# Moving the regrouping of k and q and the order of the loads in an attention and mixer kernel

## The chip, the core and the metric

The kernel runs on one core of a Trainium2 chip. Its time is the device time of one execution in microseconds (us). A comparison takes the median of several runs. The five engines of the core each work through a list of instructions in the order written: PE (the matrix engine, with its weight loads shown apart as PEld), DVE (the vector engine), ACT (the scalar engine), POOL (GpSimd) and SP, which here only issues transfers. An instruction waits at the head of its list until what it reads is there and what it overwrites is free, and all that stands behind it on that engine waits with it.

## What is computed

Sigmoid attention over 8 batches, 12 heads, 448 positions and 64 values a head, followed by a mixer block on the result:

```python
scores = (1 / sqrt(64)) * matmul(q, k.transpose(0, 1, 3, 2)) - log(448)
attn_out = matmul(1 / (1 + exp(-scores)), v)          # [8, 12, 448, 64]
x = attn_out.transpose(0, 2, 1, 3).reshape(8, 448, 768)
h = maximum(x.transpose(0, 2, 1) @ w_tok1, 0) @ w_tok2
u = x + h.transpose(0, 2, 1)
out = u + maximum(u @ w_ch1, 0) @ w_ch2               # float32
```

`w_tok1` is 448x256, `w_tok2` 256x448, `w_ch1` 768x1536 and `w_ch2` 1536x768.

## The kernel before

**Cycles.** The work runs in 24 cycles, `c = 3 * b + u`: batch `b` from 0 to 7, and `u` from 0 to 2, each a unit of four heads. In cycle `c` PE makes the scores of unit `c` (seven calls of `qk`, one for each `j`), the values of unit `c - 1` (`av`), the token step of unit `c - 2` (`tok_tail`, `tok1`, `ytrans`), and, as filling between them, the channel step of an earlier batch: the second product of batch `b - 2` in every cycle (`ch2_pair`, `pieces_last`) and the first product of batch `b - 1` at the end of each third cycle (`sevens`). This steady order holds from cycle 9 (`ONE_RUN`) on. Cycles 6 to 8 go through the same steps with a list `pending` of pieces of the channel step of batch 0 (`work`), and what comes before is an opening of its own. The schedule is written out by hand: the order of calls in the program is the order on each engine.

**How k and q get to PE.** `load` (lines 110 to 118) is issued on POOL, as two transfers a tensor and batch, which also turn float32 into float16; the bytes land in `raw_k`, `raw_q` (one buffer each) or `raw_v` (two). `relayout` (120) copies a unit of `raw_k` or `raw_q` into `rel_k` or `rel_q` on DVE, three copies a tensor and batch. `dma_transpose` (138) is one transfer from SP that transposes the three units into `tr_k` or `tr_q`, which `qk` reads. `through_dma` (144) gives the eight pieces of a batch as a list: three copies and the transpose of k, then three copies and the transpose of q. The list `copies` is emptied at places that the code names: in the steady cycles `some(within)` stands after the third `qk`, ahead of `av`, and `some(behind)` stands after the channel step's `rest()`, ahead of `ytrans`.

**What else stands on DVE.** `av` ends in two copies `xa` to `xT` (line 220) and a small one (226); `ytrans` (305) ends in the two additions to `ut` (319); `rest` ends in additions into `outs` (564); `sevens` has the additions and the clamp at lines 521 and 524; `token_sums` (434) makes four tiles `diffs` a batch. The first two matter here: `av` and `ytrans` both use the PSUM banks 0 and 1 (`at_bank[0] = Y`), and so does `tok_tail`. The next user of a bank waits on PE until DVE (or ACT, for `tk`) has emptied it.

**What else stands on SP.** The transpose of `xT` into `xn` (`xtrans_dma`, 235), that of `ut` into `un` (`utrans`, 324), and the stores.

**When the loads go out.** `gated_loads(b)` (969) is called near the end of a batch's second or third cycle. Its first instruction is a small copy on POOL that reads the last piece of `tr_q` of batch `b + 1`, so POOL waits until that transpose has landed and then issues `load` for v of batch `b + 1` and for k and q of batch `b + 2`. Line 1038 does a like thing once, at the end of cycle 5. In the steady cycles the calls are at line 1144 (cycle 11) and at line 1167 (cycles 13, 16, 19).

**In the last batch** (`b == 7`) there is no batch to follow, and `copies` holds twelve sums of `c2` made on DVE (`output_sums`, 620) for the last part of the program.

Of the kernel before, what the change touches and what calls it, by code (L numbers as in the profile page):

```python
# [23 lines left out]
NU = 3  # L24
# [6 lines left out]
def kernel(  # L31
# [11 lines left out]
    nc = tc.nc  # L43

    B, H, S, E = q.shape
# [24 lines left out]
    gate = pc.tile([128, 2], FP16, name="gate")  # L70
# [24 lines left out]
    att, xn, h1, un = {}, {}, {}, {}  # L95
# [14 lines left out]
    def load(b, t, src, u0, u1):  # L110

        for g in range(2):
            dst = raw_tile(b, t)[64 * g : 64 * g + 64, u0:u1, :, :, :]
            heads = src[b, 6 * g + 2 * u0 : 6 * g + 2 * u1]
            nc.gpsimd.dma_start(
                out=dst.rearrange("p u hi j e -> p (u hi) (j e)"),
                in_=heads.rearrange("h (p j) e -> p h (j e)", j=NJ),
            )
# [25 lines left out]
    def through_dma(b, u0):  # L144

        pieces = []
        for t in ("k", "q"):
            for u in range(u0, NU):
                pieces.append(lambda t=t, u=u: relayout(b, t, u))
            pieces.append(lambda t=t: dma_transpose(b, t, u0))  # L150
        return pieces
# [27 lines left out]
    def qk(b, u, j):  # L179
        att[b, u, j] = pa.tile([128, 2, S], FP16, tag="att", bufs=10, name=f"att_{b}_{u}_{j}")  # L180
        ps = pp.tile([128, 2, 512], FP32, tag="qk", bufs=2, name=f"qk_{b}_{u}_{j}")
        for g in range(2):
            for hi in range(2):
                nc.tensor.matmul(  # L184
                    out=ps[64 * g : 64 * g + 64, hi, 0:S],
                    lhsT=tr[b, "k"][64 * hi : 64 * hi + 64, u, j, 64 * g : 64 * g + 64],
                    rhs=tr[b, "q"][64 * hi : 64 * hi + 64, u, :, 64 * g : 64 * g + 64],
                    start=True,
                    stop=True,
                )  # L190
        nc.scalar.activation(  # L191
            out=att[b, u, j][:, :, :],
            in_=ps[:, :, 0:S],
            func=SIGMOID,
            bias=bias_t[:, :],
            scale=att_scale,
        )
# [37 lines left out]
    def xtrans_dma(b, u):  # L235
        nc.sync.dma_start_transpose(
            out=xn_tile(b, u).rearrange("s g t d -> s (g t) d"),
            in_=xTs[b % 2][:, u, :, :].rearrange("d g s -> d (g s)"),
        )
# [65 lines left out]
    def ytrans(b, u, banks=()):  # L305
        for g in range(2):
            db = NU * g + u
            if banks:
                at_bank[0] = banks[g]
            ps = bank([128, 512], FP32, f"yt_{b}_{db}")  # L310
            for tcb in range(2):
                nc.tensor.matmul(  # L312
                    out=ps[:, 0:S],
                    lhsT=h1[b, u][:, tcb, g, :],
                    rhs=w2[:, tcb, :, :],
                    start=(tcb == 0),
                    stop=(tcb == 1),
                )
            nc.vector.tensor_tensor(  # L319
                out=uts[b % 2][:, db, 0:S], in0=xTs[b % 2][:, u, g, 0:S], in1=ps[:, 0:S], op=ADD  # L320
            )
# [79 lines left out]
    def weight_sums():  # L401

        low, high = slice(0, NU), slice(NU, NDB)
        first, second = slice(0, MC), slice(MC, CC)
        s1, s2, s4 = sums

        def one(out, in0, in1, op):
            return [
                lambda d=d: nc.vector.tensor_tensor(
                    out=out[:, d, :], in0=in0[:, d, :], in1=in1[:, d, :], op=op  # L410
                )
                for d in range(NU)
            ]

        return [
            *one(s1, c1[:, high, second], c1[:, low, second], ADD),
            *one(s2, s1, c1[:, low, first], SUB),
            *one(s4, c1[:, high, first], s2, SUB),
            *one(c1[:, low, second], c1[:, low, first], c1[:, low, second], SUB),
        ]  # L420
# [350 lines left out]
    for g, queue in enumerate((nc.scalar, nc.sync)):  # L771
        queue.dma_start(
            out=first_q[64 * g : 64 * g + 64].rearrange("p hi j e -> p hi (j e)"),
            in_=q[0, 6 * g : 6 * g + 2].rearrange("h (p j) e -> p h (j e)", j=NJ),
# [28 lines left out]
    for par in range(2):  # L803
        part = slice(64 * par, 64 * par + 64)
        nc.gpsimd.dma_start(
            out=w1[part, 0:3, :],
            in_=tok_rows[0:6].rearrange("(t par) p c -> par p t c", par=2)[par],
# [161 lines left out]
    def gated_loads(b):  # L969

        nc.gpsimd.tensor_copy(  # L971
            out=gate[:, :], in_=tr[b + 1, "q"][:, NU - 1, NJ - 1, 126:128]
        )
        if b > 1:
            load(b + 1, "v", v, 0, NU)
        for t, src in (("k", k), ("q", q)):
            if b + 2 < B:
                load(b + 2, t, src, 0, NU)

    ON_DMA = range(N_FIRST, N_CYCLES)  # L980

# [68 lines left out]
                copies.pop(0)()  # L1050

    pending, copies = [], []
    early = weight_sums()
    lane = [0]
    for c in range(2 * NU, ONE_RUN):
        b, u = divmod(c, NU)
        before, ahead = divmod(c - 1, NU), divmod(c - 2, NU)


        if c == 2 * NU:  # L1060
            first = c
            pending, shares = [*pieces_ch2(0, by_half[2:]), *pieces_last(0)], [10, 10, 10]
            total = sum(w for w, f in pending)
            spent = 0

        def work(share):
            goal = 3 * sum(shares[: c - first]) + share * shares[c - first]
            done = 0
            while pending and spent + done < total * goal / 90:
                w, f = pending.pop(0)  # L1070
                if len(pending) % 4 == 3:
                    lane[0] ^= 1
                at_bank[0] = 2 + lane[0]
                f()
                done += w
                if copies:
                    copies.pop(0)()
                elif early:
                    early.pop(0)()
            return done  # L1080

        qk(b, u, 0)
        qk(b, u, 1)
        at_bank[0] = 0
        av(*before)
        xtrans_dma(*before)
        qk(b, u, 2)
        if c == 2 * NU + 2:
            copies += through_dma(3, 0)[NU + 1 :]
        spent += work(1)  # L1090
        qk(b, u, 3)
        qk(b, u, 4)
        at_bank[0] = 0
        tok_tail(*ahead)
        tok1(*ahead, with_scores=True)
        if c == 2 * NU + 1:
            copies = through_dma(3, 0)[: NU + 1]
        spent += work(2)
        if c == 2 * NU + 2:
            utrans(b - 1)  # L1100
            token_sums(b - 1)
        qk(b, u, 5)
        qk(b, u, 6)
        if u < 2:
            at_bank[0] = 0
            ytrans(*ahead)
        spent += work(3)
        if u == 2:
            sevens(b - 1)
            at_bank[0] = 0  # L1110
            ytrans(*ahead)
            gated_loads(b)
    assert not copies and not pending and not early

    def some(n):
        for f in copies[:n]:
            f()
        del copies[:n]

    for c in range(ONE_RUN, N_CYCLES):  # L1120
        b, u = divmod(c, NU)
        before, ahead = divmod(c - 1, NU), divmod(c - 2, NU)
        if b == NU:
            within, behind = ((0, 0), (4, 2), (2, 0))[u]
        else:
            within, behind = 2, 2
        if u == 0:
            assert not copies
            copies += through_dma(b + 1, 0) if b + 1 < B else output_sums()

        X, Y = 2, 0
        at_bank[0] = X
        turn0, turn1, rest = ch2_pair(b - 2, u)
        part = len(turn1) * 2 // 3
        qk(b, u, 0)
        qk(b, u, 1)
        for f in turn0:
            f()  # L1140
        qk(b, u, 2)
        some(within)
        if c == ONE_RUN + 2:
            gated_loads(b)
        if u == 2:
            utrans(b - 1)
        at_bank[0] = Y
        av(*before, 0, 4)
        qk(b, u, 3)
        av(*before, 4, NJ)  # L1150
        xtrans_dma(*before)
        if u == 2:
            token_sums(b - 1)
        qk(b, u, 4)
        for f in turn1[:part]:
            f()
        qk(b, u, 5)
        for f in turn1[part:]:
            f()
        at_bank[0] = Y  # L1160
        tok_tail(*ahead)
        qk(b, u, 6)
        tok1(*ahead, with_scores=True)
        rest()
        some(behind)
        if u == 1 and NU < b < B - 1:
            gated_loads(b)
        if u == 2:
            at_bank[0] = Y + 1
            for w, f in pieces_last(b - 2):  # L1170
                f()
            sevens(b - 1)
        at_bank[0] = Y
        ytrans(*ahead)
    assert not copies


# [90 lines left out]
```

## The time and the profile before

| | |
|---|---|
| runs | 345.99, 347.44, 349.06 us; median 347.44 us |
| profiled execution | 347.11 us, of which the span from the first to the last instruction is 345.3 us |
| busy share of the span | PEld 70%, DVE 62%, ACT 61%, POOL 16% |
| loads from POOL | 41.5% of the 16 transfer engines' time |
| transposes and stores from SP | 49.2% of it |
| waits of PE for another engine, all together | 2.5 us |
| waits of POOL for `tr_q` to land (its gate copies) | 153.0 us at line 971, 14.0 us at line 1038 |
| one copy of `relayout` (line 126) | 611 ns alone, 1.14 us for two in a row |
| one addition to `ut` (line 319) | 614 ns alone, 1.15 us for two in a row |

In the profile a line of a timeline gives the start, the duration, the engine, the line of the program, the operation with what it writes and reads, how many in a row, and in brackets how long the engine had sat idle before and who released it. The ends of the matrix instructions are modelled, and an instruction of PE that waits for its bank can be shown as a longer one. So a wait of PE is better read from the distance between the starts of like steps in two cycles than from PE's idle time.

### The profile page before, as it was taken

The page shows a single profiled execution, that of the slowest core. Times are in us where ns is not written, and L with a number is a line of the kernel's source. Part 1 is how long each engine was busy: PE and PEld are TensorE (multiplying, and loading weights), DVE is VectorE, ACT ScalarE, POOL GpSimd, SP SyncE. Part 2 cuts the span into 40 slices and gives each one's busy share as a digit, 9 for nine tenths or more (in the row PEclk, how much of TensorE's full clock was granted, in tenths as well). Part 3 has the DMA queues.
Part 4 walks back from the last instruction along what each step waited for, and adds up shares of the span by engine and source line. Part 5 has one row for each costly group of instructions (what it writes and reads, how often), then busy time and mean ns, then how long its engine had stood idle before and what let it go on. Part 6 is the DMA issues. An engine that isn't in the chain of part 4 may idle for free.

```text
span 345.3 us, 10256 instructions
## 1 busy us (share of the span) xinstructions
PE 338.2 (98%) x4465; PEld 241.5 (70%) x4465; DVE 213.7 (62%) x427; ACT 210.9 (61%) x271; POOL 56.7 (16%) x98
## 2 busy tenths in 40 slices
PE   7999999999999999999999999999999999999994
PEld 4555556555886679766896669766896779767962
DVE  2377466577775665756575654765665684976662
ACT  3996846487748865788448865688448875111400
POOL 8982440230040013000400013000100000000000
PEclk9999999999999999999999999999999999999999
DMA  7999999999999999989997999979963592035406
GB/s 120 174 170 189 208 203 203 169 175 219 200 181 205 198 184 208 153 126 164 181 228 87 165 193 156 199 108 170 176 135 30 82 171 68 1 78 128 79 2 159
DMA packets 104380, 52.17 MB, mean 151 GB/s; under 512 B 76432, under 2 KB 101264, under 8 KB 104336
## 3 DMA queue, kind: packets, MB, share of 16 engines
q1 hardware_dynamic: 78944, 29.70, 49.2%
q0 software_dynamic: 25168, 21.50, 41.5%
q8 instruction: 35, 0.57, 0.7%
q10 hardware_dynamic: 224, 0.33, 0.4%
q14 instruction: 9, 0.07, 0.1%
HBM read 43.45 MB, written 11.01 MB: 158 GB/s over the span
## 4 chain that ended last, share of the span: by engine, by line
PE 88%; ACT 4%; DMA 3%; DVE 2%; issue 1%; POOL 0%; DVEq 0%; ACTq 0%
PE c_ab L491 14%; PE c L367 12%; PE qk L184 9%; PE c_c L491 8%; PE xa L211 8%; PE c L605 6%; PE tk L289 5%; PE c L734 5%; PE yt L312 5%; PE c L541 4%; ACT att L191 4%; PE c L695 4%; PE c L344 3%; DMA raw_k<-in_k_dram 2%; DMA first_q<-in_q_dram 1%; PE c_b L491 1%
## 5 line engine op out<-in xcount | busy, mean ns | idle before, releaser
L191 ACT ACTIVATE att<-qk,att_bias 128x896 f16<-128x896 f32 x168 | 155.3, 1015 | 34.0 <-PE qk L184 33.7
L184 PE MATMUL qk<-tr_q,tr_k 64*64 64x448 f16 x672 | 59.5, 359 | 0.3 <-ACT att L191 0.2
L491 PEld LDWEIGHTS <-c 128*128 128x128 f16 x504 | 47.8, 98 | 1.9 <-issue 1.8
L367 PE MATMUL c<-c,h 64*64 64x384 f16 x960 | 47.1, 322 | 0.0
L220 DVE CAST xT<-xa 128x448 f16<-128x448 f32 x48 | 27.7, 620 | 31.1 <-PE xa L211 31.0
L211 PE MATMUL xa<-att,raw_v 64*64 64x448 f16 x672 | 40.3, 349 | 0.1
L512 ACT ACTIVATE pt_ab<-c_ab 128x896 f32<-128x896 f32 x21 | 19.3, 917 | 30.8 <-PE c_ab L491 30.8
L367 PEld LDWEIGHTS <-h 64*64 64x64 f16 x960 | 29.5, 107 | 11.0
L491 PEld LDWEIGHTS <-sum 128*128 128x128 f16 x378 | 36.3, 98 | 0.0
L184 PEld LDWEIGHTS <-tr_k 64*64 64x64 f16 x672 | 21.5, 105 | 19.2 <-issue 11.9
L564 DVE TENSOR_TENSOR o<-un,c 128x384 f32<-128x384 f16 x34 | 18.8, 554 | 23.9 <-PE c L605 20.6
L319 DVE TENSOR_TENSOR ut<-xT,yt 128x448 f16<-128x448 f16 x48 | 27.5, 614 | 2.5 <-PE yt L312 2.5
L211 PEld LDWEIGHTS <-raw_v 64*64 64x64 f16 x672 | 21.5, 107 | 10.6 <-issue 1.0
L971 POOL COPY gate<-tr_q 128x2 f16<-128x2 f16 x6 | 1.1, 184 | 153.0 <-DMA tr_q<-rel_q 153.0
L303 ACT ACTIVATE h<-tk 128x256 f16<-128x256 f32 x42 | 14.3, 412 | 14.8 <-PE tk L289 14.8
L541 PE MATMUL c<-c,h 128*128 128x384 f16 x120 | 22.3, 326 | 0.0
L312 PE MATMUL yt<-w,h 128*128 128x448 f16 x96 | 22.1, 353 | 0.0
L605 PE MATMUL c<-c,h 128*128 128x384 f16 x120 | 22.0, 326 | 0.0
L514 ACT ACTIVATE h<-c_ab 128x896 f16<-128x896 f32 x7 | 6.4, 917 | 24.4 <-PE c_ab L491 24.4
L289 PE MATMUL tk<-xn,w 128*128 128x256 f16 x156 | 21.2, 274 | 0.1
L521 DVE TENSOR_TENSOR h<-pt_c,c_c 128x448 f16<-128x448 f32 x21 | 13.0, 617 | 13.2 <-PE c_c L491 13.2
L521 DVE TENSOR_TENSOR h<-pt_ab,c_ab 128x896 f16<-128x896 f32 x14 | 15.2, 1084 | 9.6 <-PE c_ab L491 9.6
(100 smaller groups left out, 461.4 us busy)
## 6 DMA issues: line engine op xcount, KB each, us to landing
out_dram<-o SPq DMA_DIRECT2D x48, 192.0 KB, 2.9
c<-in_moe_w_ch_dram POOLq DMA_DIRECT2D x4, 1152.0 KB, 15.9
raw_k<-in_k_dram POOLq DMA_DIRECT2D x10, 336.0 KB, 10.8
raw_q<-in_q_dram POOLq DMA_DIRECT2D x10, 336.0 KB, 13.7
raw_v<-in_v_dram POOLq DMA_DIRECT2D x10, 336.0 KB, 8.0
out_dram<-o SPq DMA_DIRECT2D x15, 96.0 KB, 6.9
raw_q<-in_q_dram POOLq DMA_DIRECT2D x12, 112.0 KB, 5.0
raw_k<-in_k_dram POOLq DMA_DIRECT2D x12, 112.0 KB, 4.8
```

Source lines behind the costliest of these rows:

```text
L184: nc.tensor.matmul(out=ps[64 * g : 64 * g + 64, hi, 0:S], lhsT=tr[b, "k"][64 * hi : 64 * hi + 64, u, j, 64 * g : 64 * g + 64], rhs=tr[b, " ...
L191: nc.scalar.activation(out=att[b, u, j][:, :, :], in_=ps[:, :, 0:S], func=SIGMOID, bias=bias_t[:, :], scale=att_scale,)
L211: nc.tensor.matmul(out=ps[g][64 * hi : 64 * hi + 64, 0:S], lhsT=raw[b, "v"][64 * g : 64 * g + 64, u, hi, j, :], rhs=att[b, u, j][64 * g : ...
L220: nc.vector.tensor_copy(out=xTs[b % 2][:, u, g, 0:S], in_=ps[g][:, 0:S])
L289: nc.tensor.matmul(out=ps[tcb], lhsT=w1[rows, t, cols], rhs=xn[b, u][rows, :, t, :], start=(t == 0 and not with_scores), stop=(t == (2 if ...
L312: nc.tensor.matmul(out=ps[:, 0:S], lhsT=h1[b, u][:, tcb, g, :], rhs=w2[:, tcb, :, :], start=(tcb == 0), stop=(tcb == 1),)
L319: nc.vector.tensor_tensor(out=uts[b % 2][:, db, 0:S], in0=xTs[b % 2][:, u, g, 0:S], in1=ps[:, 0:S], op=ADD)
L367: nc.tensor.matmul(out=ps[p][m : m + 64, 0:n], lhsT=lhsT(p, part, m), rhs=rhs(p, part), start=(first and turn == 0), stop=(last and turn = ...
L491: nc.tensor.matmul(out=ps[:, g, p, :], lhsT=weights[n][:, d, 128 * cb : 128 * cb + 128], rhs=moving[n][:, d, :], start=(n in (1, 5, 2) and ...
L521: nc.vector.tensor_tensor(out=shaped(dst), in0=shaped(parts[gs, which]), in1=ps, op=ADD)
L541: nc.tensor.matmul(out=ps[:, 0:DH], lhsT=h2[b][:, BY_GROUP[cb], 128 * t : 128 * t + 128], rhs=c2[:, BY_GROUP[cb], cols], start=(cb == 0), ...
L605: nc.tensor.matmul(out=ps[p][:, 0:DH], lhsT=h2[b][:, BY_GROUP[n], 128 * t : 128 * t + 128], rhs=c2[:, BY_GROUP[n], DH * p : DH * p + DH], ...
```

## The change

Four things are moved; no instruction of PE or ACT is added or taken away.

- In cycle 7 the first four pieces for batch 3 (three copies of k and their transpose) come into `copies` after `ytrans` and no more after `tok1`; what the cycle's last `work` does not take is done at the head of cycle 8.
- In the steady cycles `some(behind)` and the call of `gated_loads` that follows it stand behind `ytrans`. For batches 4 to 6 the pieces go to other places: k's first two copies at the end of the first cycle, its third copy and transpose within the second, and all of q at the end of the second. In batch 3 one copy of q goes from the end of the second cycle to within the third. In the last batch the counts stay as they are.
- `gated_loads` issues k, v, q instead of v, k, q, except in its call for `b == 2`, which issues v and k, and no q.
- That q, of the fifth batch (`b` is 4), is loaded in cycle 9, behind a small copy on POOL that reads the `xn` of unit 2 of batch 2, whose transpose stands directly ahead of it.

```diff
@@ gated_loads @@
-        if b > 1:
+        first, second = b == 2, b > 2
+        if first:
             load(b + 1, "v", v, 0, NU)
-        for t, src in (("k", k), ("q", q)):
-            if b + 2 < B:
-                load(b + 2, t, src, 0, NU)
+        if b + 2 < B:
+            load(b + 2, "k", k, 0, NU)
+        if second:
+            load(b + 1, "v", v, 0, NU)
+        if 2 != b < B - 2:
+            load(b + 2, "q", q, 0, NU)
@@ cycles 6 to 8 @@
+        some(len(copies))
         qk(b, u, 0)
...
         tok1(*ahead, with_scores=True)
-        if c == 2 * NU + 1:
-            copies = through_dma(3, 0)[: NU + 1]
         spent += work(2)
...
             ytrans(*ahead)
+        if c == 2 * NU + 1:
+            copies += through_dma(3, 0)[: NU + 1]
         spent += work(3)
@@ cycles from 9 on @@
         if b == NU:
-            within, behind = ((0, 0), (4, 2), (2, 0))[u]
+            within, behind = ((0, 0), (4, 1), (3, 0))[u]
         else:
-            within, behind = 2, 2
+            within, behind = ((0, 2), (2, 4), (0, 0))[u] if b < B - 1 else (2, 2)
...
         xtrans_dma(*before)
+        if c == ONE_RUN:
+            nc.gpsimd.tensor_copy(out=gate[:, :], in_=xn[before][:, 1, 3, 126:128])
+            load(b + 1, "q", q, 0, NU)
...
         rest()
-        some(behind)
-        if u == 1 and NU < b < B - 1:
-            gated_loads(b)
...
         ytrans(*ahead)
+        some(behind)
+        if u == 1 and NU < b < B - 1:
+            gated_loads(b)
```

`some(n)`, which does the next `n` pieces of `copies`, is defined ahead of cycle 6 in place of cycle 9.

More of the change, by code (lines that the diff above doesn't have):

```diff
@@ L1052, with some @@
     pending, copies = [], []
+    def some(n):
+        for f in copies[:n]:
+            f()
+        del copies[:n]
     early = weight_sums()
@@ L1113 @@
     assert not copies and not pending and not early
[L1115 to L1118, printed above, removed]
     for c in range(ONE_RUN, N_CYCLES):
```

## The prediction

> **What bounds the kernel now.** First the page, for who is busy, and for the clock.
>
> ```profile
> PE 338.2 (98%) x4465; PEld 241.5 (70%) x4465; DVE 213.7 (62%) x427; ACT 210.9 (61%) x271; POOL 56.7 (16%) x98
> ...
> PEclk9999999999999999999999999999999999999999
> DMA  7999999999999999989997999979963592035406
> ```
>
> PE is busy all through at full clock, and the transfer engines nearly so until slice 29. Which of them sets the pace is seen in the windows, one for each steady batch from the end of its first two `qk` to the same place a batch later (the third column is PE's busy time).
>
> ```profile
> 102.48:141.83 39.35, 39.35 (x583) 29.56 (x577) 24.12 (x49) 26.78 (x36) 4.13 (x7) 1.00 1.18 199
> 141.83:180.99 39.16, 39.16 (x585) 29.18 (x579) 23.88 (x48) 26.68 (x36) 4.13 (x7) 1.00 0.98 167
> 180.99:220.14 39.15, 39.15 (x583) 29.19 (x579) 23.82 (x48) 26.67 (x36) 4.13 (x7) 1.00 1.05 162
> 220.14:259.29 39.15, 39.15 (x582) 29.23 (x578) 23.76 (x48) 26.66 (x36) 1.50 (x3) 1.00 0.88 146
> ```
>
> Three batches take 39.15 us to within 0.01, with two loads fewer in the last of them: PE alone sets that pace, and DVE, ACT and the transfers follow. Only the first (batch 3) is 0.20 longer. So what the change can gain is where PE waits for DVE. The chain of waits shows that place.
>
> ```profile
> 72.50 6.09 DMA raw_k<-in_k_dram
> 78.59 0.02 issue
> 78.61 1.15 DVE rel_k L126 x2
> 79.76 0.46 DVE o L571
> 80.22 0.53 DVE rel_k L126
> 80.75 1.07 DVE ut L319 x2
> 81.81 0.04 issue
> 81.86 1.51 PE xa L211 x26
> ```
>
> In cycle 7 DVE stands at the first copy of k until the load lands; the additions to `ut` come behind it, and `av` of cycle 8 needs their bank. After that, but for batch 3 and batch 7, the chain is PE's own work.
>
> **What the change takes away.** From the first `qk` of a cycle to the channel work behind `av` it is 2.02 us in cycle 7 (72.38 to 74.40) and 2.50 in cycle 8 (80.99 to 83.49): PE lost 0.48. With k's copies behind the additions, these are made when `yt` is there, at about 79.8 to 80.95, before `av` at 81.39. The weight sums that take the copies' places in `work` are three of 0.55, in DVE's 1.51 us of waiting. Gain 0.48.
>
> In batch 3, two copies of q stand ahead of the additions, in the timeline:
>
> ```profile
> 118.33 1.14 DVE L126 COPY rel_q<-raw_q 128x896 f16<-128x896 f16 x2
> ...
> 119.39 1.14 DVE L319 TENSOR_TENSOR ut<-xT,yt 128x448 f16<-128x448 f16 x2
> ...
> 122.15 1.16 DVE L220 CAST xT<-xa 128x448 f16<-128x448 f32 x2 [1.09 <-PE xa L211]
> ```
>
> `xa` takes 0.96 for 16 there (120.57 in the chain) against 0.76 elsewhere. Gain 0.20. In batch 7 the `c2` sums stand the same way: `xa` at 269.08 and 277.46 takes 0.84. Gain 2 x 0.08 = 0.16. Together 0.84.
>
> **What it moves in batches 4 to 6, at no cost.** DVE: behind cycle 12's additions come three copies, 3 x 0.57 = 1.71. `yt` of cycle 12 starts at 148.71; the addition follows 0.67 later where nothing stands ahead (109.36 to 110.03), so it runs from 149.38 to 150.53, the copies end at 152.24, and `xT` is wanted at 153.17: cover 0.93. The border to cycle 14 is the same with q. Beyond this cover PE loses one for one, less 0.3. SP: no piece changes places with another there, but k's transpose starts 1.6 later (152.3) and q's 2.2 (161.2 for 159.0); `xn` and `un` queue behind, some 2 us late. The late `xn` (167.28 to 169.5, landing up to 12 later) is read by `tok_tail` of cycle 15, at about 185: cover over 3. POOL: the gate opens at 167.7 for 165.5. With the landings of before (9.4 for the first tensor, 14.5 for the second, 15.8 for the third, from the first load of batch 5) k is there at 178, v at 185, q at 187; their readers come at 189, 190 and 198. v has the least cover, 5 us, and PE would lose what goes beyond that. In batch 7 two sums fall into `sevens`, where DVE waits 1.95 at 291.13 ahead of its addition: 2 x 0.55 fit. In cycle 8, k's transpose starts 1.1 late (82.6) and q's up to 1.1; `tr_q` is wanted at 101.4 and lands at 97.6 at the latest: cover 3.8.
>
> **What it may cost: q of batch 4.** Before, it went out at 100.37 and had 18 us until its copy. Now it waits for `xn`. No row shows this load, so by bounds.
> - `xn` goes out at 106.97, less 0.48. It landed after 8.2 (115.2), 0.8 behind the last load (q, 114.4). Without q the last load is k, 109.4, some 0.5 later by the gate. Rows for `xn`: 3.1 with no load in flight, 8.2 with loads. I take 0.8 behind k: 110.7, nearest to the second row's manner. The load's halves go out at 111.2 and 111.9.
> - The second half of a load landed in 6.1 (k, cycle 6, beside an `xn`), 8.3 (v, cycle 8, beside a `un`) and 9.0 (v, cycle 19, beside `un` and `xn`). Beside this one flies `tr_k` (7.2). I take 8.3: landed at 120.2.
> - DVE comes to q's first copy at 119.0 (`yt` at 117.66 - 0.48, addition 0.67 later, 1.15 long), waits 1.2, copies until 121.9. `xT` is wanted at 122.15 - 0.48 - 0.20 = 121.47: 0.43 late. `tok_tail` needs its banks 0.31 after `xT` (123.31 to 123.62). So PE loses 0.1; with 6.1 nothing; with 9.0, 0.8. The added gate copy itself is 0.18 us on POOL, hidden.
>
> Sum: 0.84 - 0.12, some 0.7 less. The profiled execution took 347.11, so 346.4 by it; it is 0.33 below the median, which gives 346.7 there.
>
> **Rivals.**
> *q of batch 4 comes late (slower).* If `xn` still takes 8.2, it lands at 114.7; halves at 115.2 and 115.9, landing 9.0 later at 124.9; copies until 126.6, `xT` 5.1 late, PE loses 4.8, and the net is 4.0 slower: 351.4. For it: every `xn` beside loads took 6.6 to 11.8. Against: the loads in flight then are one fewer. The gain is gone from a landing at 121.0 on, and 1% is lost from 124.4.
> *DVE's copies hold the load up.* POOL waited 0.65 for DVE (line 524) inside q's issue at 100.37. The three copies of k run from 110.6 to 112.3, over the new issue. If they hold it to their end, the halves go out at 112.3 and 113.0, land by 121.3, copies until 123.0, `xT` 1.5 late, PE loses 1.2: 0.4 slower, 347.8. The copy takes 611 ns for 896 values where line 524 takes 0.39 us for as many, so it is not plainly of the kind that held POOL; hence little weight. [...]
> *Nothing comes of it.* The freed 0.84 turns up at the next wait, so 347.4. Against: in cycle 8 the third `qk` needs the first sigmoid's bank, free at 82.5 while PE would come at 82.7, so the cover is small but there; behind it the chain is PE's. For: with the halves at their bounds the loss to q takes it all.
> *Much faster.* If the unprofiled runs (up to 349.06) hold more of these waits than the profiled one, 3.5 or more could go: 343.9. Nothing in the trace says so.
>
> **How the numbers follow.** Forecast, with its landings up to 121.0: 0.58. Nothing comes of it: 0.15. DVE holds the load: 0.09. q late: 0.12, most of it at the far end. Much faster: 0.06. The likeliest is 346.7. The runs spread 1.5 below and 1.6 above their median, so the low end is 346.7 - 1.5 = 345.2; the high end takes in the hold-up and the start of the late case with that spread: 350.2. About 1% (3.5 us) is what a measurement of this kernel can tell from no change. Faster by more: 0.06. Slower by more: the far end of the late case, 0.11. Within: 0.83.
>
> **What would show it.** Right: the distance from `qk` to the channel work in cycle 8 at 2.02; cycle 11's `xa` x16 at 0.76; batch 7's at 0.76; batches 4 to 6 still 39.15. q's first copy in cycle 11 starting without a wait for `raw_q`, or with one under 2 us. Wrong: a wait of DVE for `raw_q` of over 2 us and `tok_tail` behind it, `rel_k` of batch 4 waiting for `raw_k`, or `av` of batch 5 waiting for `raw_v`.

## The result and the profile after

The changed kernel takes 349.89 us (median of 21 runs, 347.65 to 353.86), the kernel before 347.62 (21 runs): a ratio of 1.0076, with a 95% interval of 1.0048 to 1.0104. It is slower by 2.3 us by the medians, and by 2.6 by the ratio, which compares means and leaves out the slowest run of the changed kernel, since that is over 1.5% above its fastest. That is inside the range that was given, but on the other side of the 0.7 us less that was forecast.

The profiled execution took 349.85 us with a span of 348.1, against 347.11 and 345.3 before. First the chain of waits of the changed kernel around batch 3 (start, length, what).

```profile
110.81 1.59 DVE rel_k L126 x3
112.41 1.22 issue
113.63 0.65 POOL raw_q L115
114.28 9.60 DMA raw_q<-in_q_dram
123.88 0.02 issue
123.90 1.67 DVE rel_q L126 x3
125.57 1.07 DVE xT L220 x2
126.65 0.04 issue
126.69 0.30 PE tk L270 x2
```

Before, this stretch of the chain was PE's own. Now it runs from POOL's issue of q of batch 4 over the load to DVE and only then to PE. (The first two lines are the chain's guess at why POOL issued so late; an experiment below goes against it.) The timeline has the same with the idle times in brackets.

```profile
106.61 1.24 SPq L236 DMA_TRANSPOSE xn<-xT  x1
...
111.67 0.19 POOL L1159 COPY gate<-xn 128x2 f16<-128x2 f16 x1 [12.98 <-DMA xn<-xT]
...
113.63 1.32 POOL L115 DMA_DIRECT2D raw_q<-in_q_dram  x2 [1.76 <-issue]
...
123.90 1.67 DVE L126 COPY rel_q<-raw_q 128x896 f16<-128x896 f16 x3 [4.79 <-DMA raw_q<-in_q_dram]
124.73 0.10 PEld L270 LDWEIGHTS <-w 64*64 64x64 f16 x1 [1.70 <-DMA xn<-xT]
125.49 1.15 DVE L220 CAST xT<-xa 128x448 f16<-128x448 f32 x2
...
126.16 0.30 PE L270 MATMUL tk<-xn,w 64*64 64x256 f16 x2 [2.76 <-DVE xT L220]
```

DVE stands 4.79 us at q's first copy. `xT` starts at 125.49, though PE had finished its `xa` by 121.7, and `tok_tail` (line 270) waits for the banks that `xT` empties. (The line of PEld, which loads its weights, shows a second lateness: the `xn` that `tok_tail` reads landed at about 124.7. The wait for `xT` covers it; the third experiment comes back to it.) In batches 4 to 6 the steady pace is the old one, as the starts of the first product of each batch show in the chain of waits:

```profile
131.31 1.25 PE c_ab L491 x12
...
170.46 1.26 PE c_ab L491 x12
...
209.61 1.25 PE c_ab L491 x12
...
248.76 1.26 PE c_ab L491 x12
```

They lie 39.15 apart, as before. The account of the 2.74 us between the two profiled executions, from such distances:

| stretch | before | after | difference |
|---|---|---|---|
| opening, to the fourth `qk` of cycle 7 | 75.65 | 75.29 | -0.36 |
| from there to the first product of batch 1 | 13.32 | 13.32 | 0 |
| cycle 11, from its channel step to the first product of batch 2 (timeline) | 9.42 | 12.69 | +3.27 |
| from there to the first product of batch 6 | 156.78 | 156.60 | -0.18 |

The opening isn't touched by the change. Undelayed, cycle 11's stretch is 9.22 (seen in the first experiment), so PE loses 3.47 there. (By the chain of waits it is 9.11 undelayed and 12.59 here: 3.48.)

Cycle 8 came out even although its `av` lost its wait:

```profile
80.63 0.57 PE L184 MATMUL qk<-tr_q,tr_k 64*64 64x448 f16 x8
81.04 1.49 PE L211 MATMUL xa<-att,raw_v 64*64 64x448 f16 x28
...
82.65 1.15 PE L541 MATMUL c<-c,h 128*128 128x384 f16 x6
...
84.75 0.30 PE L270 MATMUL tk<-xn,w 64*64 64x256 f16 x4 [0.28 <-DMA xn<-xT]
```

From `qk` to the channel work it is 2.02 (80.63 to 82.65), as it should be; then `tok_tail` waits for the `xn` of cycle 7, which was issued at 75.41 and landed 9.3 us later.

### The profile page after: what moved, and what is told of

The parts are those of the page before. It is cut to its first block, busy times and chain, and to the rows that moved or that the text cites. A ratio compares the mean times of both kernels' runs of the same rounds, so it can differ in the third digit from the quotient of the medians.

```text
span 348.1 us, 10256 instructions
## 1 busy us (share of the span) xinstructions
PE 336.8 (97%) x4465; PEld 238.2 (68%) x4465; DVE 213.2 (61%) x427; ACT 210.6 (61%) x271; POOL 57.6 (17%) x99
## 4 chain that ended last, share of the span: by engine, by line
PE 79%; DMA 10%; POOL 4%; DVE 2%; ACT 2%; issue 1%; ACTq 0%; POOLq 0%
PE c_ab L491 14%; PE c L367 10%; PE c_c L491 8%; PE qk L184 7%; PE xa L211 6%; PE c L605 5%; PE c L734 5%; PE c L541 5%; PE tk L289 4%; PE yt L312 4%; PE c L695 4%; DMA c<-in_moe_w_ch_dram 3%; PE c L344 3%; DMA raw_q<-in_q_dram 3%; DMA xn<-xT 3%; DMA w<-in_moe_w_tok_dram 2%
## 5 line engine op out<-in xcount | busy, mean ns | idle before, releaser
L184 PE MATMUL qk<-tr_q,tr_k 64*64 64x448 f16 x672 | 57.7, 356 | 0.5 <-DVE tr_k L176 0.2
L211 PE MATMUL xa<-att,raw_v 64*64 64x448 f16 x672 | 39.6, 349 | 0.0
L367 PEld LDWEIGHTS <-h 64*64 64x64 f16 x960 | 28.1, 107 | 11.9
L184 PEld LDWEIGHTS <-tr_k 64*64 64x64 f16 x672 | 20.6, 105 | 19.9 <-issue 12.3
L211 PEld LDWEIGHTS <-raw_v 64*64 64x64 f16 x672 | 20.3, 107 | 10.8 <-issue 0.3
```

Source lines behind the costliest of these rows:

```text
L184: nc.tensor.matmul(out=ps[64 * g : 64 * g + 64, hi, 0:S], lhsT=tr[b, "k"][64 * hi : 64 * hi + 64, u, j, 64 * g : 64 * g + 64], rhs=tr[b, " ...
L211: nc.tensor.matmul(out=ps[g][64 * hi : 64 * hi + 64, 0:S], lhsT=raw[b, "v"][64 * g : 64 * g + 64, u, hi, j, :], rhs=att[b, u, j][64 * g : ...
L367: nc.tensor.matmul(out=ps[p][m : m + 64, 0:n], lhsT=lhsT(p, part, m), rhs=rhs(p, part), start=(first and turn == 0), stop=(last and turn = ...
```

## The experiments

The theory: q of batch 4 lands too late, DVE waits for it at the head of its list, and the emptying of PE's banks stands behind. The main rivals: the later regrouping or the new order of the loads costs something by itself; the late transfer slows the transposes that PE needs.

**One part undone.** q of batch 4 goes out with v and k again.

```diff
-        if 2 != b < B - 2:
+        if b < B - 2:
             load(b + 2, "q", q, 0, NU)
...
-        if c == ONE_RUN:
-            nc.gpsimd.tensor_copy(out=gate[:, :], in_=xn[before][:, 1, 3, 126:128])
-            load(b + 1, "q", q, 0, NU)
```

> The changed kernel with one part undone: q of batch 4 goes out with v and k at the end of cycle 8 again, and the small gate copy of cycle 9 is gone. Theory (that load lands too late, DVE waits for it at the head of its list, and the emptying of the value banks stands behind): no wait of DVE for raw_q in cycle 11, from its channel work to the first product of batch 2 it is 9.11 us again and not 12.6, and the time is 0.2 to 0.9 below the kernel before, 346.7 to 347.4. Rival (the later regrouping and the order k, v, q cost something themselves): the time stays 1 us or more above the kernel before.

Measured: 347.20 us (12 runs) beside 348.06 of the kernel before, ratio 0.9971 (0.9939 to 1.0003). The chain of waits has cycle 11's stretch at 9.11:

```profile
119.21 1.30 PE c L367 x32
...
128.32 1.25 PE c_ab L491 x12
```

So this one part is what makes the change slower, and the rest costs nothing that these runs can tell: the first rival falls. Whether the rest gains anything, the interval leaves open. (Its profile lost 0.29 in cycle 10, where `tok_tail` waited for an `xn` that took 8.55 us to land.)

**That part alone, in the kernel before.**

```diff
-            if b + 2 < B:
+            if b + 2 < B and (b, t) != (2, "q"):
                 load(b + 2, t, src, 0, NU)
...
         xtrans_dma(*before)
+        if c == ONE_RUN:
+            nc.gpsimd.tensor_copy(out=gate[:, :], in_=xn[before][:, 1, 3, 126:128])
+            load(b + 1, "q", q, 0, NU)
```

> The kernel before with this one part added: q of batch 4 is loaded in cycle 9 behind xn. Its first two copies then stand ahead of the additions to ut too. Theory: DVE waits for raw_q from about 118.3 until the load lands at 122 to 125, additions and xT come behind it, PE loses 4 to 7 us in cycle 11, and the time is 351 to 354. Rival (the move is free by itself, another part costs): 347.6, as before.

Measured: 353.84 us (4 runs) beside 348.06, ratio 1.0139 (1.0085 to 1.0192). In the timeline DVE waits 4.88 for the load, the additions to `ut` come behind it, and `av` waits for their banks:

```profile
123.96 1.14 DVE L126 COPY rel_q<-raw_q 128x896 f16<-128x896 f16 x2 [4.88 <-DMA raw_q<-in_q_dram]
...
125.02 1.14 DVE L319 TENSOR_TENSOR ut<-xT,yt 128x448 f16<-128x448 f16 x2
125.69 2.23 PE L211 MATMUL xa<-att,raw_v 64*64 64x448 f16 x16 [4.45 <-DVE ut L319]
```

So the change's copies behind the additions do soften the late load: here a landing 4.2 us after the start of cycle 11's channel step costs PE 7.68 us in cycle 11 (by the chain), there one after 5.16 costs 3.48. The time is in the range expected, the loss of PE above it. Part of the 7.68 is not waiting at all: 16 `xa` take 2.23 for the usual 0.93, and the granted clock is 0.50 there (last section).

**The load as late, its copies behind `xT`.**

```diff
-            within, behind = ((0, 0), (4, 1), (3, 0))[u]
+            within, behind = ((0, 0), (4, 0), (0, 0))[u]
...
-        if c == ONE_RUN + 2:
-            gated_loads(b)
...
         xtrans_dma(*before)
+        if c == ONE_RUN + 2:
+            some(4)
+            gated_loads(b)
```

> The changed kernel with the load of q as late as it is, but all its copies stand in cycle 11 behind the copies to xT. Theory (the place in DVE's list is what costs, not the transfer): DVE still waits for raw_q up to about 124, but tok_tail no longer waits for xT; PE loses at most 0.5 there, and the time is 346.8 to 347.8. Rival (the late transfer itself slows the transposes that PE needs): cycle 11 stays 2 us or more too long and the time at 349 or above.

Measured: 347.92 us (12 runs) beside 348.06, ratio 0.9987 (0.9954 to 1.0019): most of the loss is gone with the load at its late place (issued at 113.07, landed by 123.2). But cycle 11 still lost 1.1 us, since `tok_tail` now waited for the `xn` of cycle 10:

```profile
113.12 5.44 SPq L139 DMA_TRANSPOSE tr_k<-rel_k  x1
...
118.66 4.19 SPq L236 DMA_TRANSPOSE xn<-xT  x1
...
124.98 0.30 PE L270 MATMUL tk<-xn,w 64*64 64x256 f16 x4 [0.92 <-DMA xn<-xT]
```

SP took 5.44 to issue the transpose of k beside the load (3.75 in the kernel before), `xn` came out behind it and landed after 6.29 (4.0 before). The time is just above the theory's range, and the loss of 1.1 lies between the 0.5 at most of the theory and the 2 of the rival, so each has a part: DVE's list carries the larger, the slowed transposes a smaller one that the larger hid. The changed kernel's own profile has it hidden: there the transpose of k went out 1.2 us ahead of the load and took SP only 3.23, but `xn` behind it landed 8.9 us after its issue at 115.78, about 1.5 us later than `tok_tail` would have wanted it.

**k's copies and transpose of batch 4 later**, so that neither runs beside the load.

```diff
-            within, behind = ((0, 0), (4, 1), (3, 0))[u]
+            within, behind = ((0, 0), (0, 4), (4, 0))[u]
```

> The changed kernel with the copies and the transpose of k of batch 4 at the end of cycle 10 and all of q within cycle 11, so that no copy of DVE runs when POOL comes to the load of q. If DVE's copies held POOL: from the end of the gate copy to the load 0.3 to 0.7 us (1.76 in the changed kernel). If not: still 1.2 or more. The load then goes out at about 112.2 and lands at 120 to 122; DVE comes to it at about 120.8, so PE loses 0 to 1.5 in cycle 11 and the time is 346.9 to 348.6.

Measured: 346.86 us (10 runs) beside 348.06, ratio 0.9968 (0.9936 to 0.9999).

```profile
110.64 0.18 POOL L1159 COPY gate<-xn 128x2 f16<-128x2 f16 x1 [11.16 <-DMA xn<-xT]
112.59 1.31 POOL L115 DMA_DIRECT2D raw_q<-in_q_dram  x2 [1.77 <-issue]
...
118.97 1.66 DVE L126 COPY rel_k<-raw_k 128x896 f16<-128x896 f16 x3
120.55 1.66 DVE L126 COPY rel_q<-raw_q 128x896 f16<-128x896 f16 x3
```

The load's second half lands in 7.1 us without the transpose of k beside it, and DVE, which has k's copies to do first, doesn't wait for it. Cycle 11 is 9.29 by the chain. Two things help here at once, the faster landing (at 120.3) and q's later place on DVE: with the 9.6 us of the changed kernel the load would have landed at 122.8 and DVE would have waited some 2 us (an estimate). But the gap ahead of the load is 1.77 again with no copy of DVE near (DVE is idle from 110.76 to 113.40): DVE's copies are not what holds POOL there.

**The gate on `xT` and not on `xn`.**

```diff
-            nc.gpsimd.tensor_copy(out=gate[:, :], in_=xn[before][:, 1, 3, 126:128])
+            nc.gpsimd.tensor_copy(out=gate[:, :], in_=xTs[before[0] % 2][:, before[1], 1, 510:512])
```

> The changed kernel, but the small copy on POOL ahead of the load of q of batch 4 reads xT of unit 2 (written by DVE at about 106.5) and not xn (landed at 111.5), so that the load goes out earlier. Theory (lateness of the landing decides): the load goes out between 106.8 and 108.5, lands before 118.5, DVE doesn't wait for raw_q, cycle 11 is 9.1 us again, and the time is 346.7 to 347.6. Rival (where the load is called in the list matters, not when it goes out): still 349 or more.

Measured: 346.82 us (10 runs) beside 348.09, ratio 0.9983 (0.9956 to 1.0010). The load goes out 1.74 after its gate copy here too, later than was expected, but 2.0 behind the issue of `xn` and not 7.0 as in the changed kernel; its second half lands in 6.9, DVE doesn't wait, and cycle 11 is 9.11 by the chain. When the load lands decides, not where it is called. (The profiled run, 348.77, is the slowest of the ten for another reason: `tok_tail` of cycle 7 waited 2.44 for an `xn` issued in cycle 6, ahead of all that the change moves.)

**More tiny copies on POOL,** four and then 24, behind the loads of cycle 8, to find what holds the load.

```diff
+        for _ in range(4 if first else 0):
+            nc.gpsimd.tensor_copy(out=gate[:, :], in_=ident[:, 126:128])
```

> The changed kernel with four more tiny copies on POOL behind the loads of cycle 8, to settle what holds the load of q after its gate copy (1.76 us in the changed kernel, and 1.77 in all looks at this load behind xn, with DVE's copies beside it and without). If the hold belongs to a place in POOL's list of instructions (such as the reading of the next stretch of it), it moves by four instructions into POOL's idle time, the load goes out 0.3 to 0.7 after the gate copy, lands some 1.4 earlier, and PE loses 1 to 2.5 in cycle 11: 348 to 349.3. If it belongs to this gate and load, it stays 1.77, and so does the time, 349.5 to 350.5.

> As with four more tiny copies on POOL behind the loads of cycle 8, but 24, for the same question with a larger step: if the hold of 1.75 us ahead of the late load of q belongs to a place in POOL's list, that place now lies among the tiny copies, and the load goes out 0.3 to 0.7 behind its gate copy. If it belongs to the load itself, it is 1.7 to 1.8 again. The time says nothing here; the gap in the timeline does.

Measured: with four, 351.84 us (10 runs) beside 348.09, ratio 1.0068 (1.0026 to 1.0111), gap 1.78; the time is above the 349.5 to 350.5 expected, and the last section has a cause for it. With 24 (one run, 347.96):

```profile
98.76 6.18 POOL L982 COPY gate<-ident 128x2 f16<-128x2 f16 x24
...
109.73 0.18 POOL L1161 COPY gate<-xn 128x2 f16<-128x2 f16 x1 [4.79 <-DMA xn<-xT]
...
111.68 1.33 POOL L115 DMA_DIRECT2D raw_q<-in_q_dram  x2 [1.77 <-issue]
...
121.98 1.67 DVE L126 COPY rel_q<-raw_q 128x896 f16<-128x896 f16 x3 [3.06 <-DMA raw_q<-in_q_dram]
```

The gap stays, so it belongs to this load behind this gate, not to a place in POOL's list. What it is stays open: it is 1.74 to 1.78 in all eight traces that have this load (in two of them the profile puts it down to DVE, in six to nothing that it shows), and behind the gates of line 971 the first load comes after 0.27 to 0.35 (once, at 70.84 in the changed kernel, right behind a gate copy of 0.54). In this run `xn` happened to land early, and the load landed at 121.96 and not 123.88, that is 3.44 and 5.16 after cycle 11's channel step began; PE lost 1.76 and 3.48. So 1.72 of landing make 1.72 of PE's time: one for one.

**The first part of the change alone,** the copies of k of batch 3 behind the additions in cycle 7.

```diff
-        if c == 2 * NU + 1:
-            copies = through_dma(3, 0)[: NU + 1]
         spent += work(2)
...
             ytrans(*ahead)
+        if c == 2 * NU + 1:
+            copies += through_dma(3, 0)[: NU + 1]
```

> The kernel before with one part of the change alone: the copies of k of batch 3 behind the additions to ut in cycle 7. Prediction's own account: av of cycle 8 loses its wait, 0.48 us, and the time is 0.3 to 0.6 below the kernel before. Rival from the looks so far: tok_tail of cycle 8 waits for xn instead, the distance from the third qk of cycle 7 to the first product of batch 1 stays 13.2 to 13.4 us, and the time is within 0.2 of the kernel before.

Measured: 347.27 us (12 runs) beside 349.21 for the kernel before, whose runs spread from 345.85 to 351.29 here; ratio 0.9972 (0.9941 to 1.0002). In its timeline the fourth `qk` of cycle 7 starts at 75.81 and the first product at 88.65: 12.84, not 13.32, the whole 0.48. `tok_tail` started at 84.82 without a wait. In the changed kernel's profile the same gain went into the wait for `xn`. Eight traces have this part of the change with the token step in its old place. From the first `qk` of cycle 8 to the first product they take 7.50, 7.50 and 7.57 in three, and 7.89 to 8.24 in the five in which `tok_tail` waits for `xn`. Without this part it is 7.98 in the kernel before and 8.53 in the second experiment, whose load of k landed later. So the gain is there when `xn` lands early enough, and it is given back, all or in part, when not; its size changes from run to run with both landings.

**Both kernels beaten?** The kernel with k's copies later, with one more edit: in cycle 8 the token step stands behind the second stretch of channel work.

```diff
-        tok_tail(*ahead)
-        tok1(*ahead, with_scores=True)
+        if u < 2:
+            tok_tail(*ahead)
+            tok1(*ahead, with_scores=True)
         spent += work(2)
+        if u == 2:
+            at_bank[0] = 0
+            tok_tail(*ahead)
+            tok1(*ahead, with_scores=True)
```

> The kernel with the later copies of k, and in cycle 8 the token step stands behind the second stretch of channel work. Looked for: whether the gain of the moved copies in cycle 8 was taken back by the wait of tok_tail for xn. If so, tok_tail no longer waits there, cycle 8 is 0.3 to 0.6 shorter from its first qk to the first product of batch 1, and the time is 346.2 to 346.7. If another wait comes in its place: 346.9 as without it.

Measured: 346.70 us (12 runs) beside 348.09, ratio 0.9967 (0.9935 to 1.0000), the lowest median of all. In cycle 8 `tok_tail` no longer waits (85.75), and from the fourth `qk` of cycle 7 to the first product it is 12.97 (75.54 to 88.51), 0.35 less than in the changed kernel. Against the kernel with k's copies later alone (0.9968) the difference can't be told. Both are clear of the changed kernel; against the kernel before the intervals end at 1.

## Why the prediction was wrong

- **The bound and the steady batches.** Right. Batches 4 to 6 stay at 39.15 with every load later and in another order; no wait for `raw_k` or `raw_v` appears there.
- **Gain in cycle 8, 0.48.** The mechanism was right and shown by the part alone; in the changed kernel's profile it came to nothing, for the reason that the third rival named (it turns up at the next wait). The next wait was `xn`, not the sigmoid that the prediction looked at.
- **Gains in batches 3 and 7, 0.20 and 0.16.** Right: `xa` x16 stood unstalled in cycle 11, in batch 7 it takes 0.76 both times (271.99 and 280.29 in the chain), and the stretch to batch 6 is 0.18 shorter.
- **The cost of q of batch 4, 0.1.** This is the step that failed. The mechanism (DVE at the head of its list, then `xT`, then the banks of `tok_tail`) was the right one, and its size was wrong: DVE waited 4.79 and not 1.2, and PE lost 3.48 and not 0.1. The landing was put at 120.2 and came at 123.88. Three terms of that sum were too small. The load went out 1.96 after the gate opened (the 1.76 gap and the gate copy) where 0.5 was put, which is what the loads behind the gates of line 971 take. Its second half took 9.6 where 8.3 was taken, the middle of three rows, since the transpose of k flies beside it (9.3 to 10.3 in the five traces with it, 6.9 to 7.3 in the three in which k's transpose came 3 us or more behind). These two come back in every trace. The third is chance in part: the gate opened at 111.67 where `xn` was put at 110.7. It had taken 4.9 us from its issue where 4.2 was put, and in the seven traces of this gate it took 3.2 to 5.7. With the earliest of them (the run with 24 tiny copies) PE still lost 1.76.
- **The rivals.** "q of batch 4 comes late" was what happened, at its right place: its rule, a loss of PE of what `xT` is late less 0.3, gives 3.4 for the 3.7 that `xT` was late (125.49, where the first experiment's distances put it at 121.76), and 3.48 was measured. A chance of 0.12 was little for it. It was tied to one cause, `xn` landing after 8.2, which none of the seven traces shows, and the lateness came from smaller terms that add up. "DVE's copies hold the load up" gave a hold of 1.1 where 1.46 was measured, for a wrong reason.
- **The chances.** The move is within the 1% that they go by; with 21 runs of each kernel, 0.76% could be told from none all the same.

## What to carry to other kernels

A step that is moved behind a new wait should be costed with all terms of its new path at their late rows together, and put against the cover once more: where a delay of 0.8 us takes the whole gain and three terms of the path can each be 1 us longer, the late case is not the rare one. A copy that waited for a load at the head of DVE's list cost here what stood behind it, so ask first what that is: with a load about as late, PE lost 7.7 us (some 2.8 of them, by the estimate of the last section, to a granted clock of 0.50), 3.5 and 1.1 as the copies stood ahead of the additions, ahead of `xT` and behind it; the last is what the slowed transposes cost. And a wait removed on the busiest engine was a gain only as far as the next thing it needed was early: the 0.48 of cycle 8 was kept whole where `xn` had landed (12.84 for 13.32), and in the changed kernel the stretch stayed at 13.32.

## What the runs showed of the hardware

In the second experiment PE lost more than it waited: 7.68 us, of which it stood 4.45. The windows of that run (length, busy times of PE, PEld, DVE, ACT and POOL, then the granted clock, DMA share and GB/s):

```profile
121.00:123.00 2.00, 0.24 (x8) 0.00 (x0) 0.00 (x0) 1.48 (x2) 0.00 (x0) 1.00 1.01 145
123.00:125.00 2.00, 0.00 (x0) 0.00 (x0) 1.04 (x2) 0.00 (x0) 0.00 (x0) 0.88 1.30 194
125.00:127.00 2.00, 1.31 (x14) 0.63 (x17) 1.69 (x4) 0.00 (x0) 0.00 (x0) 0.50 1.04 249
127.00:129.00 2.00, 2.00 (x28) 1.28 (x24) 0.00 (x0) 0.61 (x1) 0.00 (x0) 0.50 0.58 109
129.00:131.00 2.00, 2.00 (x31) 1.33 (x27) 1.88 (x5) 1.40 (x2) 0.00 (x0) 0.50 1.17 216
131.00:133.00 2.00, 2.00 (x36) 1.40 (x26) 1.33 (x3) 1.28 (x2) 0.00 (x0) 0.91 1.42 93
```

PE had stood some 3.3 us since its last work at 121.24 when the clock fell from 1.00 to 0.50 at 124.5 (an estimate from the rows: 0.88 is 1.52 us at 1.00 and 0.48 at 0.50), and it stayed there until about 131.4: 6.8 us in all, the last 5.7 of them with PE at work again. At half clock that is some 2.8 us more (an estimate), over a third of the 7.68. The profiled run of the kernel with four tiny copies on POOL, whose cycle 11 is that of the changed kernel with a load 0.5 us later, has it too:

```profile
123.00:125.00 2.00, 1.99 (x48) 1.17 (x40) 0.00 (x0) 2.00 (x4) 0.00 (x0) 1.00 1.43 210
125.00:127.00 2.00, 0.00 (x0) 0.10 (x1) 1.01 (x2) 0.73 (x1) 0.00 (x0) 1.00 0.74 208
127.00:129.00 2.00, 0.52 (x8) 0.24 (x7) 1.97 (x6) 0.00 (x0) 0.00 (x0) 1.00 0.03 6
129.00:131.00 2.00, 2.00 (x15) 1.15 (x10) 1.80 (x4) 1.56 (x3) 0.00 (x0) 0.66 1.15 216
131.00:133.00 2.00, 2.00 (x8) 0.79 (x8) 0.69 (x2) 0.00 (x0) 0.00 (x0) 0.50 1.07 194
133.00:135.00 2.00, 2.00 (x25) 1.17 (x22) 0.41 (x1) 0.00 (x0) 1.55 (x4) 0.99 1.17 216
```

PE stood 3.25 and 0.23 us there (together the 3.48 that these rows leave free); by the same working the clock fell at 129.64, 1.4 us after PE had begun again at 128.25, and came back at 133.04. These 3.4 us at half clock are some 1.7 of the 5.60 us that PE lost (an estimate). So the clock fell while PE stood in the one run, and in the other when PE was at work again after two shorter waits. In the changed kernel's profile PE stood 2.76 and 0.23 us and the clock stayed at 1.00. What decides whether it falls, and for how long, these three profiles do not show.

The runs of the changed kernel spread with the mean clock: nine, the profiled one among them, have 0.997 or more and take 347.65 to 349.89, and twelve have 0.990 to 0.995 and take 348.85 to 353.86. Of the 74 runs of the kernel before that were taken beside the experiments, only ten have 0.995 or less. The two profiles above have 0.990 with 6.8 us at half clock and 0.995 with 3.4. So a good part of the 2.3 us between the medians is likely this lower clock on top of the waiting; without traces of those runs it is not shown for them.
